# A fused attention and mixture-of-experts kernel: VectorE and GpSimd put in program order in the dense layers, with a shorter leaky step

## Chip, core and metric

The kernel runs on one core of a Trainium2 chip. The metric is the device time of one execution in microseconds (us); lower is better. TensorE multiplies, VectorE (DVE in the profile), ScalarE (ACT) and GpSimd (POOL) work element by element, and SyncE (SP) issues the transfers from memory.

## What is computed

Three stages follow each other on 2176 tokens of width 512.

```python
# 1 attention between 512 tokens and 32 state rows, 4 batches x 8 heads
xread = softmax(x @ state.T / 8) @ state;  sread = softmax(state @ x.T / 8) @ x
x = concat([xread, sread])                 # 4 * (512 + 32) = 2176 tokens, 512 wide
# 2 a dense two-layer net, 2048 hidden units, a leaky step with one slope a unit
h = x @ w_in
g = max(h, 0) + alpha * min(h, 0)
x = g @ w_out
# 3 eight experts of 1024 hidden units, weighted by P from 8 rounds of row and column scaling
out = sum(P[:, e:e+1] * (max(x @ w1[e], 0) @ w2[e]) for e in range(8))
```

Everything is float32. The kernel keeps the precision with two halves of each number: `hi` is a rounded copy that TensorE takes, `lo` is the rest, and each product is three matmuls (`hi` by `lo`, `hi` by `hi`, `lo` by `hi`). So every operand of TensorE costs one copy (ScalarE) and one subtraction (VectorE or GpSimd).

## The kernel before

The dense net, stage 2, is cut along its hidden units into 8 units `u` of 256 (two halves `f` of 128), and along the tokens into 5 chunks `c`: four of 512 tokens and a last one (c = 4, `CS`) of 128 state tokens. `program` (lines 805 to 813) lists the work as pairs: `layer1` of one chunk, then `layer2_first` of the chunk before it. A full chunk has two groups of six matmuls in `layer1` (one for each `f`) and four groups of six in `layer2_first` (one for each quarter `d` of the output). After each such group `run` calls `slot()`, which advances each of the side tasks ("lanes") by one step; a generator that yields n sleeps n slots. So a chunk is six slots, and a round of one `u` is 30.

What a chunk needs besides TensorE: `layer1` leaves a PSUM bank `ps` (three banks of the pool `ps_h`). ScalarE makes `r` = relu(h) and `v` = relu(-h) from it (lines 517, 518), VectorE makes `r` = r - alpha*v (line 519, the leaky step), and the closure `halves` makes `gh` on ScalarE (line 524) and `gl` on GpSimd (line 525). `halves` waits in the list `later` and is emitted one group of matmuls on. `layer2_first` leaves its sum in a bank of `ps_o` (three banks); VectorE adds it to `acc` (line 555; for u = 0 ScalarE copies, line 553). This is called the eviction of `d`. A bank can be filled again only after its eviction.

Two side tasks run under it. The lane "w" turns the weights of the next unit, which arrive as 64-bit numbers, into float32 and splits them: four pieces a round, each with `to_f32` (VectorE line 106, ScalarE 109 and 110, VectorE 112 and 115, GpSimd 118, VectorE 120) and `split_w` (ScalarE 135, GpSimd 136), and `load_next` issues the next transfer on SP. The lane "v" (`make_v`) multiplies the first layer's weights of the next unit by the attention's state, so that `layer1` can take the softmax weights as its input; it fills a bank of `ps_a` (two banks) and puts out two halves with `put_x` (ScalarE line 227, VectorE line 228).

Order: up to the entry (1, 2, 0) of `program` a planner orders all engines by a cost model of its own. From there on TensorE and ScalarE run in the order in which the code emits their instructions (`manual_schedule`, line 1038), while the planner still chooses the order of VectorE and GpSimd. Only in stage 3 (`experts`, line 1048) is VectorE in emitted order as well. Whatever chose the order, it is fixed before the run, and an engine takes its instructions one after the other.

Of the kernel before, what the change touches and what calls it, by code (L numbers as in the profile page):

```python
# [8 lines left out]
F32 = mybir.dt.float32  # L9
# [10 lines left out]
P = 128  # L20
# [24 lines left out]
def body(ctx: ExitStack, tc: tile.TileContext, xt_in, xn_in, stb, stk, wd, ws, alpha, wgate, out):  # L45
# [22 lines left out]
    ones = const.tile([P, P], F32, name="ones")  # L68
    rebias = const.tile([P, 1], F32, name="rebias")
    alpha_sb = const.tile([P, F1 // P], F32, name="alpha_sb")  # L70
    nalpha = const.tile([P, F1 // P], F32, name="nalpha")
    wg_raw = const.tile([P, KD, E], F32, name="wg_raw")
# [24 lines left out]
    def to_f32(u, j):  # L97
# [16 lines left out]
        )  # L114
        nc.vector.tensor_scalar(  # L115
            out=y.bitcast(I32), in0=y, scalar1=4095.0, scalar2=float(1 << 19), op0=ALU.min, op1=ALU.mult
        )
        nc.gpsimd.tensor_tensor(out=lo_w, in0=y.bitcast(I32), in1=lo_w, op=ALU.add)  # L118
# [184 lines left out]
    def read_state(b):  # L303
# [3 lines left out]
        for g in range(2):  # L307
            r2 = r2s[g]
            nc.vector.tensor_scalar(out=r2, in0=r2, scalar1=EPS, scalar2=None, op0=ALU.add)
            nc.vector.reciprocal(out=r2, in_=r2)  # L310
            nc.vector.tensor_scalar(out=a2[g], in0=a2[g], scalar1=r2, scalar2=None, op0=ALU.mult)
        yield 1
# [152 lines left out]
    def make_v(u):  # L465
# [4 lines left out]
        for bp in range(2):  # L470
# [3 lines left out]
            for j in range(2):  # L474
                ps = ps_a.tile([P, 2, NF, P], F32, tag="a", name=f"pv{u}_{bp}_{j}")
                for g in range(2):
                    k = 2 * g + j
                    for i, (s, w) in enumerate(((0, wl_t), (0, wh_t), (1, wh_t))):
                        nc.tensor.matmul(
                            ps[:, g], lhsT=st2[s][:, bp, g, j].rearrange("p h c -> p (h c)"),  # L480
                            rhs=w[u][:, :, k * P:(k + 1) * P], start=(i == 0), stop=(i == 2),
                        )
                for half in range(2):
                    h = slice(half * 64, half * 64 + 64)
                    v = v_of(u, 2 * bp + (half ^ j))
                    src = ps[h].rearrange("p g f c -> p g (f c)")
                    put_x(v[0][h], v[1][h], src)
                if j == 1:
                    v_done.add((u, bp))
                yield 2  # L490

    v_done = set()

    def layer1(u, c, f):
# [16 lines left out]
        for i, (w, x) in enumerate(terms):  # L511
            nc.tensor.matmul(ps, lhsT=w, rhs=x, start=(i == 0), stop=(i == len(terms) - 1))  # L512
        hi, lo = gh[:, f, :n], gl[:, f, :n]
        fa = u * NF + f
        r = tp.tile([P, S], F32, tag="r", name=f"r{u}_{c}_{f}", bufs=2)[:, :n]
        v = tp.tile([P, S], F32, tag="v", name=f"v{u}_{c}_{f}", bufs=1)[:, :n]
        nc.scalar.activation(out=r, in_=ps, func=AF.Relu)  # L517
        nc.scalar.activation(out=v, in_=ps, func=AF.Relu, scale=-1.0)  # L518
        nc.vector.scalar_tensor_tensor(  # L519
            out=r, in0=v, scalar=nalpha[:, fa:fa + 1], in1=r, op0=ALU.mult, op1=ALU.add  # L520
        )

# [3 lines left out]

        later.append(halves)

    def layer2_first(u, c, d):
# [7 lines left out]
        for f in range(NF):  # L537
            for wt, g in ((wh_t, gl), (wh_t, gh), (wl_t, gh)):
# [3 lines left out]
                i += 1  # L542
        for g, there, here in places(c):
            if g not in acc:
                new_acc(g)
            if c < CS:
                a, src = acc[g][:, d, there], ps[:, here]
            elif d == KD - 1:
                a, src = acc[g][:, :, there], po_t[False].rearrange("p (d n) -> p d n", d=KD)
            else:  # L550
                continue
            if u == 0:
                nc.scalar.activation(out=a, in_=src, func=AF.Copy)
            else:
                nc.vector.tensor_tensor(out=a, in0=src, in1=a, op=ALU.add)  # L555

# [258 lines left out]
    made = {}  # L815
    later, lanes = [], {"x": [], "state": [], "gate": [], "early": [], "sums": [], "blocks": [], "v": [], "w": []}
    wait = dict.fromkeys(lanes, 0)

    def advance(lane):
# [8 lines left out]
        return False  # L828

    def slot():  # L830
        for lane in lanes:
            if wait[lane] > 0:
# [33 lines left out]
    def weights(u, converted=0, first=5):  # L866

        yield first
        for j in range(NPIECE):
            if j >= converted:  # L870
                for _ in to_f32(u, j):
                    yield 1
                yield 2
            split_w(u, j)
            load_next(u, j)
            yield 2

# [15 lines left out]
    def start():  # L893
# [4 lines left out]
        nc.vector.memset(ones, 1.0)  # L898
        nc.vector.memset(rebias, -14336.0)
        warm(10)  # L900
        load_b(1)
# [16 lines left out]
        warm(30)  # L918
        nc.vector.tensor_scalar(out=nalpha, in0=alpha_sb, scalar1=-1.0, scalar2=None, op0=ALU.mult)
        lanes["x"] += [x0, x1, read_x(2), read_x(3)]  # L920
# [10 lines left out]
    def run(program):  # L931
        for kind, u, c in program:
            if kind == 1:
# [24 lines left out]
                for f in range(NF):  # L958
                    layer1(u, c, f)
                    while len(later) > 1:  # L960
                        later.pop(0)()
                    slot()
# [4 lines left out]
            else:  # L967
                while later and c == 0 and u == 0:
                    later.pop(0)()
                while (u, NPIECE - 1) not in split:  # L970
# [6 lines left out]
                for i in range(KD):  # L977
                    layer2_first(u, c, i)
                    if i == 1 and later:
                        later.pop(0)()  # L980
                    slot()
                while later:
                    later.pop(0)()
                if u == U1 - 1:
# [53 lines left out]
    with tc.manual_schedule(engines={mybir.EngineType.PE, mybir.EngineType.Activation}):  # L1038
        run(program[i:])
        flush("w")  # L1040
# [60 lines left out]
```

## Time and profile before

| | us |
|---|---|
| median of 3 runs | 1923.8 |
| lowest and highest of them | 1923.53, 1924.28 |
| the profiled execution, its own time | 1931.88 |
| span of that execution, first to last instruction | 1930.0 |
| stage 2 from `layer1` of u = 2 to the first matmul of stage 3 (177.3 to 477.5 of the span) | 300.2 |
| TensorE's matmuls over the span | 1852.3 busy, 96% |
| VectorE, ScalarE, GpSimd over the span | 64%, 39%, 64% busy |

The profiled execution took 8 us more than the median of the runs. Times inside it are counted from the span's start. Matmuls overlap each other, so a matmul's duration (0.39 us) is longer than the distance to the next one's start, and a busy TensorE is not yet one at its peak: what it needs is read from the distance between starts.

### The profile page before, as it was taken

Reading aid. Unit: us, or ns where it says so; the run is one execution under the profiler, and the core shown is the slowest. Engines: PE = TensorE matmul, PEld = TensorE weight load, DVE = VectorE, ACT = ScalarE, POOL = GpSimd, SP = SyncE. Lnnn points to the kernel's source line nnn. Section 1 sums busy time; section 2 is a strip of 40 time slices with the busy share of each in tenths; the row PEclk is TensorE's granted clock in tenths of the full one; section 3 lists DMA queues with packets and bytes.
Section 4 is the critical chain, followed back from the end, with each engine's and each line's share of the span. In section 5 each row is a group of like instructions: output and inputs, shape, how many; then the busy total and the mean of one; then the engine's idle time right before and its main releaser. Section 6 shows DMA issues by size and latency. Waiting matters only on the chain.

```text
span 1930.0 us, 26030 instructions
## 1 busy us (share of the span) xinstructions
PE 1852.3 (96%) x9544; PEld 1629.8 (84%) x9544; DVE 1229.7 (64%) x2048; ACT 756.3 (39%) x1389; POOL 1232.1 (64%) x1429
## 2 busy tenths in 40 slices
PE   7799898889989999999999999999999999999998
PEld 6687777767778989888889898888888898998997
DVE  6845777766586555556675555555566766666665
ACT  5656545554323333333343333333333333333332
POOL 4524444464756666666676666666666788888883
PEclk8799999999999999999999999999999999999999
DMA  5111111101112111221222222112221322222221
GB/s 213 44 50 55 43 36 43 44 22 33 61 50 66 66 66 67 72 70 66 70 80 92 66 66 66 66 66 67 75 67 55 121 78 80 84 87 78 77 88 50
DMA packets 66848, 132.53 MB, mean 69 GB/s; under 512 B 7712, under 2 KB 32800, under 8 KB 66720
## 3 DMA queue, kind: packets, MB, share of 16 engines
q1 hardware_dynamic: 66720, 130.86, 20.6%
q8 instruction: 75, 1.23, 0.3%
q14 instruction: 53, 0.43, 0.1%
HBM read 126.38 MB, written 4.46 MB: 68 GB/s over the span
## 4 chain that ended last, share of the span: by engine, by line
PE 80%; DVE 8%; ACT 3%; issue 3%; POOL 2%; DMA 0%; ACTq 0%; POOLq 0%; DVEq 0%
PE po L770 38%; PE py L711 14%; PE px L711 10%; PE pz L711 10%; PE po L539 3%; PE ph L512 3%; DVE r L519 2%; POOL raw L118 1%; ACT v L518 1%; DVE acc L555 1%; DVE raw L112 1%; PE psr L326 1%; DVE raw L120 1%; ACT r L517 1%; DVE y L115 1%
## 5 line engine op out<-in xcount | busy, mean ns | idle before, releaser
L792 DVE SCALAR_TENSOR_TENSOR oa<-po,pr,oa 128x512 f32<-128x512 f32 x509 | 382.0, 751 | 402.4 <-PE po L770 401.6
L648 POOL TENSOR_TENSOR wsl<-sum,wsh 128x256 fp32r<-128x256 f32 x384 | 282.9, 767 | 385.8 <-ACT wsh L646 362.1
L722 ACT ACTIVATE g2h<-c 128x384 fp32r<-128x384 f32 (+1 forms) x288 | 146.2, 508 | 849.1 <-DVE c L718 849.1
L770 PE MATMUL po<-w2h,g2h 128*128 128x512 f32 x1088 | 430.1, 395 | 0.0
L770 PE MATMUL po<-w2l,g2h 128*128 128x512 f32 x1088 | 429.6, 395 | 0.0
L770 PE MATMUL po<-w2h,g2l 128*128 128x512 f32 x1088 | 425.6, 391 | 1.2 <-DVE g2l L723 1.2
L648 POOL TENSOR_TENSOR w2l<-rw,w2h 128x512 fp32r<-128x512 f32 x192 | 247.8, 1310 | 10.4 <-ACT w2h L646 10.4
L770 PEld LDWEIGHTS po<-w2l,g2h 128*128 128x128 f32 x1088 | 204.3, 188 | 44.6
L770 PEld LDWEIGHTS po<-w2h,g2l 128*128 128x128 f32 x1088 | 204.6, 188 | 27.8 <-DVE g2l L723 1.7
L770 PEld LDWEIGHTS po<-w2h,g2h 128*128 128x128 f32 x1088 | 204.3, 188 | 24.7
L648 POOL TENSOR_TENSOR wal<-rw,wah 128x256 fp32r<-128x256 f32 x288 | 210.9, 759 | 0.0
L711 PE MATMUL px<-rB,wah 128*128 128x384 f32 (+1 forms) x768 | 189.0, 328 | 0.0
L711 PE MATMUL py<-rT,wsh 128*128 128x384 f32 (+1 forms) x768 | 188.8, 328 | 0.0
L525 POOL TENSOR_TENSOR gl<-r,gh 128x512 fp32r<-128x512 f32 (+1 forms) x80 | 92.2, 1155 | 150.0 <-ACT gh L524 142.6
L723 DVE SCALAR_TENSOR_TENSOR g2l<-c,g2h 128x384 fp32r<-128x384 f32 (+1 forms) x288 | 183.4, 637 | 0.1
L718 DVE TENSOR_TENSOR u<-py,p 128x384 f32<-128x384 f32 (+1 forms) x192 | 102.8, 535 | 118.0 <-PE py L711 52.7
L539 PE MATMUL po<-gl,wh 128*128 128x512 f32 (+1 forms) x320 | 124.1, 388 | 42.7 <-DVE acc L555 24.3
L711 PEld LDWEIGHTS px<-rB,wah 128*128 128x128 f32 x768 | 138.9, 189 | 14.0
L711 PEld LDWEIGHTS py<-rT,wsh 128*128 128x128 f32 x768 | 138.5, 189 | 8.5 <-DVE u L718 0.2
L658 POOL TENSOR_TENSOR sum<-rw 128x256 f32<-128x256 f32 x192 | 139.9, 748 | 6.2 <-DMA rw<-in_ws_dram 5.5
L711 PE MATMUL px<-rB,wal 128*128 128x384 f32 (+1 forms) x384 | 125.8, 328 | 2.8 <-POOL wal L648 2.8
L711 PE MATMUL py<-rT,wsl 128*128 128x384 f32 (+1 forms) x384 | 125.9, 328 | 0.0
(188 smaller groups left out, 3506.0 us busy)
## 6 DMA issues: line engine op xcount, KB each, us to landing
rw<-in_ws_dram SPq DMA_DIRECT2D x96, 512.0 KB, 3.5
rw<-in_ws_dram SPq DMA_DIRECT2D x96, 256.0 KB, 2.8
rw<-in_ws_dram SPq DMA_DIRECT2D x192, 128.0 KB, 2.7
raw<-in_wd_dram SPq DMA_DIRECT2D x29, 512.0 KB, 3.5
xt<-in_xt_dram SPq DMA_DIRECT2D x8, 512.0 KB, 8.1
xn<-in_xn_dram SPq DMA_DIRECT2D x16, 256.0 KB, 2.9
out_dram<-oa SPq DMA_DIRECT2D x16, 256.0 KB, 3.4
early_a<-in_wd_dram SPq DMA_DIRECT2D x2, 512.0 KB, 9.9
```

The lines of the kernel that those rows point to most:

```text
L512: nc.tensor.matmul(ps, lhsT=w, rhs=x, start=(i == 0), stop=(i == len(terms) - 1))
L519: nc.vector.scalar_tensor_tensor(out=r, in0=v, scalar=nalpha[:, fa:fa + 1], in1=r, op0=ALU.mult, op1=ALU.add)
L525: nc.gpsimd.tensor_tensor(out=lo, in0=r, in1=f32(hi), op=ALU.subtract)
L539: nc.tensor.matmul(ps, lhsT=w2(wt, u, f, d * P, P), rhs=g[:, f, :n], start=(i == 0), stop=(i == 3 * NF - 1))
L648: nc.gpsimd.tensor_tensor(out=lo[:, i], in0=src[:, i], in1=f32(hi[:, i]), op=ALU.subtract)
L658: nc.gpsimd.tensor_tensor(out=out, in0=x, in1=y, op=op)
L711: nc.tensor.matmul(bank[b], lhsT=w[:, k * P:(k + 1) * P], rhs=xf[:, j, k, :], start=(first and i == 0), stop=(i == 5), skip_group_check=True,)
L718: nc.vector.tensor_tensor(out=temp(name, tag, bufs), in0=bank[b], in1=t[x], op=ALU.add)
L722: nc.scalar.activation(out=hi, in_=src, func=AF.Relu)
L723: later.append(lambda: nc.vector.scalar_tensor_tensor(out=lo, in0=src, scalar=0.0, in1=f32(hi), op0=ALU.max, op1=ALU.subtract))
L770: nc.tensor.matmul(ps, lhsT=x[:, f, t * P:(t + 1) * P], rhs=w[:, f, :], start=(i == 0), stop=(i == 3 * NF - 1))
L792: nc.vector.scalar_tensor_tensor(out=a, in0=ps, scalar=p, in1=a, op0=ALU.mult, op1=ALU.add)
```

## The change

The change has six parts. (1) In the dense layers from entry (1, 2, 0) on, VectorE and GpSimd run in the order in which the code emits them. (2) A list `soon` with a counter, served by `tick()` at the start of each `slot()`, takes the place of `later` in the dense layers: the leaky step is emitted one slot after its matmuls, `halves` two slots after, an eviction one slot after. (3) The leaky step reads the PSUM bank itself: ScalarE makes r = relu(-h), VectorE makes h + (1 - alpha) * r; the second ScalarE pass and the tile `v` go, and `r` has three buffers. (4) In the weights' conversion the clamp and scaling on VectorE (line 115) become two ScalarE passes. (5) Conversion steps are two slots apart, with the rests after them shortened so that a piece still takes six slots; in `make_v` both copies are emitted first and both subtractions a slot later. (6) In the attention, the scaling of `a2` (line 311) goes from VectorE to ScalarE.

```diff
-        nc.vector.tensor_scalar(
-            out=y.bitcast(I32), in0=y, scalar1=4095.0, scalar2=float(1 << 19), op0=ALU.min, op1=ALU.mult
-        )
+        nc.scalar.activation(out=y, in_=y, func=AF.Relu, scale=-1.0, bias=full)
+        nc.scalar.activation(out=y.bitcast(I32), in_=y, func=AF.Copy, scale=-float(1 << 19), bias=4095.0 * (1 << 19))
...
-            nc.vector.tensor_scalar(out=a2[g], in0=a2[g], scalar1=r2, scalar2=None, op0=ALU.mult)
+            nc.scalar.activation(out=a2[g], in_=a2[g], func=AF.Copy, scale=r2)
...
+                parts = []
                 for half in range(2):
                     h = slice(half * 64, half * 64 + 64)
                     v = v_of(u, 2 * bp + (half ^ j))
-                    src = ps[h].rearrange("p g f c -> p g (f c)")
-                    put_x(v[0][h], v[1][h], src)
+                    parts.append((v[0][h], v[1][h], ps[h].rearrange("p g f c -> p g (f c)")))
+                for hi, lo, src in parts:
+                    nc.scalar.activation(out=hi, in_=src, func=AF.Copy)
+                yield 1
+                for hi, lo, src in parts:
+                    nc.vector.tensor_tensor(out=lo, in0=src, in1=f32(hi), op=ALU.subtract)
                 if j == 1:
                     v_done.add((u, bp))
-                yield 2
+                yield 1
...
-        nc.scalar.activation(out=r, in_=ps, func=AF.Relu)
-        nc.scalar.activation(out=v, in_=ps, func=AF.Relu, scale=-1.0)
-        nc.vector.scalar_tensor_tensor(
-            out=r, in0=v, scalar=nalpha[:, fa:fa + 1], in1=r, op0=ALU.mult, op1=ALU.add
-        )
+        nc.scalar.activation(out=r, in_=ps, func=AF.Relu, scale=-1.0)
+
+        def leak():
+            nc.vector.scalar_tensor_tensor(
+                out=r, in0=r, scalar=beta[:, fa:fa + 1], in1=ps, op0=ALU.mult, op1=ALU.add
+            )
...
-        later.append(halves)
+        soon.append([1, leak])
+        soon.append([2, halves])
...
+        if c < CS or d == KD - 1:
+            soon.append([1, evict])
...
+    def tick():
+
+        for entry in list(soon):
+            entry[0] -= 1
+            if entry[0] < 0:
+                soon.remove(entry)
+                entry[1]()
+
     def slot():
+        tick()
...
                 for _ in to_f32(u, j):
-                    yield 1
-                yield 2
+                    yield 2
+                yield 1
             split_w(u, j)
             load_next(u, j)
-            yield 2
+            yield 1
...
     with tc.manual_schedule(engines={mybir.EngineType.PE, mybir.EngineType.Activation}):
-        run(program[i:])
+        with tc.manual_schedule(engines={mybir.EngineType.DVE, mybir.EngineType.Pool}):
+            run(program[i:])
+            while soon:
+                tick()
```

## Rows read from the trace of the kernel before

**Rows 1.** Stretches: from:to, length, busy (instructions) of PE, PEld, DVE, ACT, POOL, clock, DMA, GB/s
```profile
25.00:82.80 57.80, 36.51 (x146) 28.89 (x147) 48.71 (x85) 36.31 (x67) 29.51 (x24) 0.68 0.15 50
...
292.40:341.10 48.70, 43.19 (x217) 34.64 (x217) 36.80 (x56) 26.11 (x50) 21.96 (x19) 1.00 0.14 44
...
391.50:477.50 86.00, 76.21 (x369) 61.89 (x368) 57.07 (x84) 41.64 (x80) 46.73 (x46) 0.94 0.08 25
477.50:1930.00 1452.50, 1437.35 (x7377) 1287.02 (x7376) 901.73 (x1526) 496.73 (x885) 1021.01 (x1242) 1.00 0.22 72
```

**Rows 2.** TensorE's timeline: start, duration (us), line, tiles, form; idle before, releaser
```profile
308.68 0.39 PE L539 MATMUL po<-gh,wl 128*128 128x512 f32 x1
...
309.59 0.28 PE L479 MATMUL pv<-wl,sth 128*128 128x256 f32 x1
...
310.30 0.40 PE L539 MATMUL po<-gl,wh 128*128 128x512 f32 x1
...
313.20 0.28 PE L512 MATMUL ph<-xsh,wh 128*128 128x128 f32 x1
313.31 0.27 PE L512 MATMUL ph<-xsh,wl 128*128 128x128 f32 x1
```

**Rows 3.** Waits in 177.3 to 477.5: who waited for whom, total us, times, longest
```profile
ACT wh L135 <- DVE raw L120: 40.4, 15, 3.9
...
PE po L539 <- DVE acc L555: 23.2, 20, 3.0
ACT v L227 <- DVE v L228: 19.6, 12, 4.0
...
PE po L539 <- POOL gl L525: 9.3, 11, 2.2
```

**Rows 4.** The timeline of four engines before one wait of TensorE
```profile
330.41 0.62 ACT L524 ACTIVATE gh<-r 128x512 fp32r<-128x512 f32 x1
...
331.79 1.30 POOL L118 TENSOR_TENSOR raw<-y,raw 128x512 int32<-128x512 int32 x1 [0.97 <-DVE y L115]
333.05 1.27 POOL L525 TENSOR_TENSOR gl<-r,gh 128x512 fp32r<-128x512 f32 x1
333.12 1.74 DVE L120 SCALAR_TENSOR_TENSOR raw<-raw 128x512 int32<-128x512 int32 x1 [1.42 <-POOL raw L118]
...
334.90 0.68 ACT L135 ACTIVATE wh<-raw 128x512 fp32r<-128x512 f32 x1 [3.87 <-DVE raw L120]
...
335.48 0.58 ACT L517 ACTIVATE r<-ph 128x512 f32<-128x512 f32 x1
...
338.92 0.68 DVE L555 TENSOR_TENSOR acc<-po,acc 128x512 f32<-128x512 f32 x1
...
339.66 0.50 PE L539 MATMUL po<-gl,wh 128*128 128x512 f32 x1 [1.59 <-DVE acc L555]
```

**Rows 5.** Groups by line and form, 177.3 to 477.5: count, busy us, mean ns, idle before
```profile
L519 DVE SCALAR_TENSOR_TENSOR r<-v,nalpha,r 128x512 f32<-128x512 f32 x48 | 41.7, 869 | 40.0 <-ACT v L518 40.0
L112 DVE SCALAR_TENSOR_TENSOR raw<-raw 128x512 int32<-128x512 uint16 x20 | 21.7, 1087 | 1.9 <-ACT raw L109 1.7
...
L115 DVE TENSOR_SCALAR y<-y 128x512 int32<-128x512 f32 x20 | 17.0, 848 | 0.0
...
L110 ACT ACTIVATE y<-y,rebias 128x512 f32<-128x512 int32 x20 | 14.2, 711 | 0.0
```

**Rows 6.** Two lines, each 177.3 to 477.5: durations min/median/max in ns, first and last start
```profile
L115 DVE TENSOR_SCALAR y<-y x20: 415/422/1517, 184.0 to 412.7; 128x512 int32<-128x512 f32 x20
...
L120 DVE SCALAR_TENSOR_TENSOR raw<-raw x20: 692/693/1745, 185.8 to 415.8; 128x512 int32<-128x512 int32 x20
```

**Rows 7.** The page: a group (busy us, mean ns, idle), a transfer (us to landing)
```profile
L792 DVE SCALAR_TENSOR_TENSOR oa<-po,pr,oa 128x512 f32<-128x512 f32 x509 | 382.0, 751 | 402.4 <-PE po L770 401.6
...
raw<-in_wd_dram SPq DMA_DIRECT2D x29, 512.0 KB, 3.5
```

**Rows 8.** TensorE's timeline in the first microseconds
```profile
56.41 0.80 PE L539 MATMUL po<-gl,wh 128*128 128x512 f32 x1 [7.75 <-POOL gl L525]
```

More of the change, by code (lines that the diff above doesn't have):

```diff
@@ L69, in body @@
     rebias = const.tile([P, 1], F32, name="rebias")
+    full = const.tile([P, 1], F32, name="full")
     alpha_sb = const.tile([P, F1 // P], F32, name="alpha_sb")
-    nalpha = const.tile([P, F1 // P], F32, name="nalpha")
+    beta = const.tile([P, F1 // P], F32, name="beta")
     wg_raw = const.tile([P, KD, E], F32, name="wg_raw")
@@ L514, in layer1 @@
         fa = u * NF + f
-        r = tp.tile([P, S], F32, tag="r", name=f"r{u}_{c}_{f}", bufs=2)[:, :n]
-        v = tp.tile([P, S], F32, tag="v", name=f"v{u}_{c}_{f}", bufs=1)[:, :n]
-        nc.scalar.activation(out=r, in_=ps, func=AF.Relu)
-        nc.scalar.activation(out=v, in_=ps, func=AF.Relu, scale=-1.0)
-        nc.vector.scalar_tensor_tensor(
-            out=r, in0=v, scalar=nalpha[:, fa:fa + 1], in1=r, op0=ALU.mult, op1=ALU.add
-        )
+        r = tp.tile([P, S], F32, tag="r", name=f"r{u}_{c}_{f}", bufs=3)[:, :n]
+        nc.scalar.activation(out=r, in_=ps, func=AF.Relu, scale=-1.0)
[3 more added lines that the diff above has]
+            )
         def halves():
@@ L542, in layer2_first, with evict @@
                 i += 1
[L543 to L555, printed above, removed]
+        bank = po_t[c < CS]
+        def evict():
+            for g, there, here in places(c):
+                if g not in acc:
+                    new_acc(g)
+                if c < CS:
+                    a, src = acc[g][:, d, there], bank[:, here]
+                else:
+                    a, src = acc[g][:, :, there], bank.rearrange("p (d n) -> p d n", d=KD)
+                if u == 0:
+                    nc.scalar.activation(out=a, in_=src, func=AF.Copy)
+                else:
+                    nc.vector.tensor_tensor(out=a, in0=src, in1=a, op=ALU.add)
+        if c < CS or d == KD - 1:
+            soon.append([1, evict])
     po_t = {}
@@ L815, in body @@
     made = {}
-    later, lanes = [], {"x": [], "state": [], "gate": [], "early": [], "sums": [], "blocks": [], "v": [], "w": []}
+    later, soon, lanes = [], [], {"x": [], "state": [], "gate": [], "early": [], "sums": [], "blocks": [], "v": [], "w": []}
     wait = dict.fromkeys(lanes, 0)
@@ L899, in start @@
         nc.vector.memset(rebias, -14336.0)
+        nc.vector.memset(full, 4095.0)
         warm(10)
@@ L918, in start @@
         warm(30)
-        nc.vector.tensor_scalar(out=nalpha, in0=alpha_sb, scalar1=-1.0, scalar2=None, op0=ALU.mult)
+        nc.vector.tensor_scalar(out=beta, in0=alpha_sb, scalar1=-1.0, scalar2=1.0, op0=ALU.mult, op1=ALU.add)
         lanes["x"] += [x0, x1, read_x(2), read_x(3)]
@@ L959, in run @@
                     layer1(u, c, f)
-                    while len(later) > 1:
-                        later.pop(0)()
                     slot()
@@ L967, in run @@
             else:
-                while later and c == 0 and u == 0:
-                    later.pop(0)()
                 while (u, NPIECE - 1) not in split:
@@ L978, in run @@
                     layer2_first(u, c, i)
-                    if i == 1 and later:
-                        later.pop(0)()
                     slot()
-                while later:
-                    later.pop(0)()
                 if u == U1 - 1:
```

## The prediction

> **What bounds the kernel now.** Read the stretches first [rows 1]. Stage 3 keeps TensorE busy for 1437 of 1452 us; the change doesn't touch it, and it is taken as it is. The dense stage from u = 2 on (177.3 to 477.5, 300.2 us) is another matter: in one round (292.4 to 341.1) TensorE is busy for 43.2 of 48.7 us, VectorE for 36.8, ScalarE for 26.1 and GpSimd for 22.0. No engine is full; engines wait for each other.
>
> How much is lost is read from the distances between matmul starts [rows 2]. Four matmuls of 512 columns take 309.59 - 308.68 = 0.91 us, so 0.228 each and 1.37 for a slot of six; those of 128 columns start 0.11 apart; six of `make_v` take 310.30 - 309.59 = 0.71. By the loops the stage holds 864 of the first kind, 312 of the second, 20 groups of the third and 1.4 us of gate logits: 197.0 + 34.5 + 14.2 + 1.4 = 247.1 us. So 300.2 - 247.1 = **53 us are lost**, 8.8 in each of six rounds. (For one round: 96 + 48 of the first kind, 48 of the second, four groups: 41.0 us of 48.7.)
>
> The waits tell where [rows 3]: TensorE waits 23.2 us for evictions and 9.3 for `gl`; the rest is refilling after each wait, and the clock, whose mean is 0.94 between its levels of 1.2 and 2.4 GHz from 391.5 on [rows 1]. Behind the evictions stands a chain [rows 4]: GpSimd's line 118 ends at 333.09; VectorE's line 120 takes 1.74 us, since GpSimd starts `gl` beside it; ScalarE, in program order, sat idle for 3.87 us until line 120 let it do `wh`; only then come the relus; and an eviction starts at 338.92, for which TensorE waits until 339.66. Such waits for line 120 cost ScalarE 40.4 us in 15 cases, and its second copy in `make_v` waits 19.6 us for VectorE's first subtraction [rows 3].
>
> **The change, part by part.** *Work per engine.* VectorE loses line 115 (four a round at 0.848 us [rows 5]) and the leaky step, at 0.869 now, is taken at 0.751, a step of the same kind with one PSUM operand [rows 7]: 36.8 - 3.4 - 0.9 = 32.5 us of a 41.0 us round. ScalarE loses a pass (0.58 [rows 4]) for each half chunk and gains two for each piece, bounded by 0.58 and 0.711 [rows 4, 5]; the latter is taken, being the pass on the same tile: 26.1 - 8 x 0.58 - 0.6 + 8 x 0.711 = 26.6. GpSimd stays at 22.0. All three fit under 41.0, so nothing but order can hold TensorE up.
>
> The Trainium skill (Perfetto Trace Analysis, Optimizing Scalar/DVE Operations) speaks against both moves: it gives VectorE a fixed cost some 65 ns higher from PSUM than from SBUF, and says that an operation with a VectorE performance mode is faster there. By it the 48 leaky steps would cost about 3 us more, an estimate, and line 115 should stay. The rows disagree on the first (0.751 against 0.869) and on the second only partly: undisturbed, line 115 takes 0.415, but its longest took 1.517 [rows 6].
>
> *Order, steady chunk.* Leaky step, conversion and eviction now come a slot after what feeds them. Count from the end of the second half's matmuls, with their 0.17 us of pipeline: relu done at 0.8, leaky step at 1.5, `gh` (0.62) at 2.2, two conversion passes at 3.6, `gl` (1.3) at 3.5, line 118 at 4.9, line 120 (0.693 undisturbed [rows 6]) at 5.6. VectorE puts the evictions of d = 0 and 1 in between, and its next use of line 120 is ScalarE's `wh` in the next chunk, at 6.9 or later: no wait. `gl` is needed at 8.2. The 40.4 us of waiting on ScalarE go, and so does the 19.6 in `make_v`, where both copies precede both subtractions.
>
> *Order, short chunk.* After the first chunk of a round, TensorE has only 24 short matmuls (2.7 us) before the next `layer1` (2.7). ScalarE has lines 109 and 110 ahead of `gh`: `gh` of both halves at 2.8 and 3.4, the new passes at 4.8; GpSimd `gl` at 4.1 and 5.4, line 118 at 6.7; line 120 at 7.4. `gl` is just in time (needed at 5.4 and 6.1). Queued behind line 120 on VectorE are the short chunk's eviction (8.1), two leaky steps with line 106 between them (taken at 0.42 as line 115, a step of its kind: 10.0), and the eviction of d = 0 (10.7). TensorE needs that bank at 5.4 + 3 x 1.37 = 9.5: a wait of 1.2, with refilling 1.5 us.
>
> *Slots with `make_v`.* For eight slots a round, VectorE has in every two slots two subtractions, a conversion step and two evictions or leaky steps, 4 x 0.68 + 0.7 to 1.09 [rows 4, 5] = 3.4 to 3.8, against 2 x 1.37 + 0.71 = 3.44 of TensorE. Up to 0.4 too much four times; an eviction may be late by two slots less its own 0.68 and the pipeline, 1.9. Bounds 0 and 1.6 us; I take 1.0.
>
> *Sum of the stage.* A steady round keeps 1.5 + 1.0 = 2.5 of 8.8 us; four of them 10. In the last two rounds the planner's VectorE also has the block differences for stage 3, which are not moved; I leave 11 of 17.6. So 21 of 53 stay: **32 us gained** (bounds: 53, and 20 if each steady round keeps twice as much and the last two 13).
>
> *Free of cost.* The transfers that `load_next` puts on SP go out a slot (1.4 us) later; they land in 3.5 us [rows 7] and are used 13 slots on. If they had to be waited for, it would be 1.4 us a piece. The leaky step holds its PSUM bank for a slot more; the third bank covers that.
>
> *First 177 us.* Here the planner still orders everything, and no row shows its choice. Best: the longest wait goes, -7.75 [rows 8]. Worst: the eight pieces of the first two units each add 2 x 0.711 - 0.422 = 1.0 us to the path, and eight scalings of `a2` 0.62 each: +13. I take 0: from 25 to 82.8 VectorE is the fuller engine (48.7 against 36.3 [rows 1]) and is the one relieved.
>
> Against the profiled execution: 1931.9 - 32 = 1899.9 us. It stands 8 us over the median; the parts that change are the same in both, so 1923.8 - 32 = **1892 us**.
>
> **The rivals.** *A held queue on VectorE (slower).* Line 120 sits in emitted order ahead of leaky steps and evictions, and its input now hangs on two more ScalarE passes. What such a place costs an engine in fixed order is seen on ScalarE today: up to 3.9 us, 2.7 in the mean [rows 3]. If VectorE waits W at each of 20 pieces, an eviction behind it is late by W + 0.69 - 1.9. With 11 us elsewhere the stage loses more than now once 20 x (W - 1.21) + 11 > 53, so from W = 3.3 on; at 3.9 it is 65, time **1936**. For it: the short chunk comes to a wait of that kind. Against: pieces are two slots a step now, and the steady chunk shows none. The Trainium skill says of these engines that their queues are strictly first in, first out (PSUM — Partial Sum Buffer, Engine vs sequencer instructions); by that rule this rival lives.
>
> *Twice the waits.* VectorE's spare 8.5 us a round is eaten, since GpSimd's steps lengthen lines 106, 112 and 120 (line 112 takes 1.087 in the mean [rows 5]) in the full slots. Rounds keep 5 and the last two 14: 34 of 53, **1905**.
>
> *All waits go.* The short chunk is eased because ScalarE's passes take 0.58, and the last rounds gain as the others: 6 of 53 stay, **1877**.
>
> *It does not do what it says.* The planner's order was near the emitted one, and what counted was the chain's length: one pass (0.58) less for `gl`, but 1.42 - 0.85 more for line 118. These cancel: **1923**.
>
> **How the numbers follow.** Forecast 0.50, all waits go 0.17, twice the waits 0.16, no effect 0.06, held queue 0.11. Faster by over 0.2% (about what a measurement of this kernel can tell from no change): 0.83; within: 0.06; slower: 0.11. The range leaves out the held queue and the far ends: low 1923.8 - 53 = 1871, high 1923.8 - 20 + 13 = 1917.
>
> **What the profile would show.** Right: rounds of some 43.5 us where they were 48.7; ScalarE's wait for line 120 below 15 us; no leaky step over 0.8 us; one wait for an eviction of about 1.2 us left a round, in the chunk after the short one; stage 3 as long as before. Wrong: VectorE idle before line 120 for over 3 us a piece, with evictions behind it; or a start that lasts past 183 us to `layer1` of u = 2.

## The result, and the profile after

The changed kernel takes 1893.8 us (median of 4 runs, 1891.8 to 1898.4) against 1924.0 us: a ratio of 0.984, 95% interval 0.982 to 0.987. The forecast was 1892 us with a range of 1871 to 1917. The profiled execution is the slowest of the four, 1898.44 us, with a span of 1896.7. The profiled execution of the kernel before is 8 us above its median too, so the two spans differ by 33.3 us and the medians by 30.2.

The stretches of the changed kernel, in the columns of [rows 1]. Stage 2 from `layer1` of u = 2 now runs from 180.9 to 447.3.

```profile
25.00:82.80 57.80, 34.27 (x148) 28.68 (x149) 39.01 (x65) 41.32 (x77) 24.48 (x20) 0.66 0.15 50
...
238.60:281.20 42.60, 41.37 (x217) 35.17 (x216) 31.03 (x52) 27.11 (x49) 22.18 (x19) 1.00 0.15 50
...
366.40:447.30 80.90, 74.55 (x369) 60.90 (x368) 52.95 (x81) 37.96 (x69) 48.75 (x47) 0.96 0.09 27
447.30:1896.70 1449.40, 1434.44 (x7377) 1284.33 (x7375) 900.92 (x1526) 496.89 (x885) 1023.48 (x1242) 1.00 0.22 72
```

A round went from 48.7 us (the one in [rows 1]; they vary from 48.3 to 50.0) to 42.6, the stretch that ends stage 2 from 86.0 to 80.9, and stage 3 from 1452.5 to 1449.4 [rows 1]. Over the span: the start is 3.6 us longer (180.9 against 177.3), stage 2 is 33.8 us shorter (266.4 against 300.2), stage 3 is 3.1 us shorter; together 33.3, the difference of the spans.

Two lines give all of stage 2, before and after:

```profile
177.30:477.50 300.20, 266.00 (x1305) 214.59 (x1304) 217.26 (x319) 156.22 (x298) 141.99 (x123) 0.97 0.12 37
```

```profile
180.90:447.30 266.40, 254.01 (x1305) 213.19 (x1305) 186.11 (x298) 156.03 (x277) 143.94 (x123) 0.99 0.13 42
```

TensorE's idle time fell by 21.8 us (34.2 to 12.4), and the same matmuls were busy for 12.0 us less. Part of that is the clock: it stood at 1.2 GHz for 17.1 us of stage 2 before and for 6.8 us after. Matmuls of 512 columns then start 0.43 us apart (428.48 and 428.90 in the changed kernel) in place of 0.228, so about half of such a stretch is lost: an estimate of 5 of the 33.8 us.

The waits of the changed kernel in stage 2 (who waited for whom, total us, times, longest), to be laid beside [rows 3]:

```profile
DVE raw L121 <- POOL raw L119: 33.9, 10, 4.3
ACT wh L136 <- DVE raw L121: 30.4, 15, 2.5
...
PE po L547 <- DVE acc L564: 10.8, 8, 2.7
...
PE po L547 <- POOL gl L532: 1.6, 3, 0.7
```

TensorE's waits fell from 23.2 + 9.3 to 10.8 + 1.6 us. But ScalarE still waits 30.4 us for line 120 (121 in the new file), where it waited 40.4. So that wait, with which the prediction's reading of the chain began, is mostly still there, and TensorE's waits fell all the same.

One wait of TensorE is left in each round. Here are TensorE's and VectorE's timelines before it (start, duration, line, tiles, idle before):

```profile
271.30 0.28 PE L547 MATMUL po<-gh,wl 128*128 128x128 f32 x1
...
279.71 0.50 PE L547 MATMUL po<-gl,wh 128*128 128x512 f32 x1 [1.23 <-DVE acc L564]
```

```profile
275.32 0.69 DVE L121 SCALAR_TENSOR_TENSOR raw<-raw 128x512 int32<-128x512 int32 x1 [4.29 <-POOL raw L119]
275.93 0.68 DVE L564 TENSOR_TENSOR acc<-po,acc 128x512 f32<-128x512 f32 x1
276.53 0.74 DVE L526 SCALAR_TENSOR_TENSOR r<-r,beta,ph 128x512 f32<-128x512 f32 x1
277.19 1.21 DVE L107 TENSOR_SCALAR y<-raw 128x512 int32<-128x512 int32 x1
278.32 0.73 DVE L526 SCALAR_TENSOR_TENSOR r<-r,beta,ph 128x512 f32<-128x512 f32 x1
278.98 0.68 DVE L564 TENSOR_TENSOR acc<-po,acc 128x512 f32<-128x512 f32 x1
```

It is the queue that the prediction wrote out for the short chunk: the conversion step held for GpSimd, then the short chunk's eviction, two leaky steps with a conversion step between them, and the eviction for which TensorE stands still for 1.23 us. VectorE keeps its order: the short chunk's last matmul started at 271.30 and took 0.28 us, but its eviction stood behind line 121 and ran at 275.93.

The leaky step, one line of each kernel, durations min/median/max in ns (the first fence is the kernel before, the second the changed one):

```profile
L519 DVE SCALAR_TENSOR_TENSOR r<-v,nalpha,r x60: 339/752/1799, 180.1 to 465.2; 128x512 f32<-128x512 f32 x48, 128x128 f32<-128x128 f32 x12
```

```profile
L526 DVE SCALAR_TENSOR_TENSOR r<-r,beta,ph x60: 336/737/750, 183.2 to 435.0; 128x512 f32<-128x512 f32 x48, 128x128 f32<-128x128 f32 x12
```

None of the 60 is over 0.750 us, though GpSimd worked beside 32 of them for more than 0.1 us; before, the longest took 1.799, and all 15 steps over 0.8 us had GpSimd at work beside them. The Trainium skill (SBUF — State Buffer, Who interferes with whom) says that a VectorE instruction with at most one input in SBUF, outside the two-port modes, does not contend with GpSimd, and that one with two inputs there contends with a GpSimd instruction that reads SBUF. The trace agrees.

### The profile page after: what moved, and what is told of

It reads as the page before. It is cut to its first block, busy times and chain, and to the rows that moved or that the text cites. A ratio compares the mean times of both kernels' runs of the same rounds, so it can differ in the third digit from the quotient of the medians.

```text
span 1896.7 us, 25997 instructions
## 1 busy us (share of the span) xinstructions
PE 1838.0 (97%) x9544; PEld 1628.7 (86%) x9544; DVE 1192.9 (63%) x2009; ACT 765.1 (40%) x1381; POOL 1235.6 (65%) x1429
## 3 DMA queue, kind: packets, MB, share of 16 engines
q8 instruction: 75, 1.23, 0.3%
## 4 chain that ended last, share of the span: by engine, by line
PE 87%; DVE 5%; POOL 2%; ACT 2%; issue 2%; DMA 1%; SPq 0%; POOLq 0%; ACTq 0%; DVEq 0%
PE po L782 39%; PE py L723 15%; PE px L723 10%; PE pz L723 10%; PE po L547 7%; PE ph L518 4%; PE pv L480 1%; PE psr L327 1%; POOL gl L532 1%; POOL raw L119 1%; DVE r L526 1%; PE psc L248 1%; DMA raw<-in_wd_dram 1%; DVE acc L564 0%; DVE y L107 0%
## 5 line engine op out<-in xcount | busy, mean ns | idle before, releaser
L547 PE MATMUL po<-gl,wh 128*128 128x512 f32 (+1 forms) x320 | 121.1, 379 | 12.4 <-DVE acc L564 10.8
```

The costliest lines, as they stand in the source:

```text
L547: nc.tensor.matmul(ps, lhsT=w2(wt, u, f, d * P, P), rhs=g[:, f, :n], start=(i == 0), stop=(i == 3 * NF - 1))
```

## The experiments

The theory of the prediction was "order": no engine is full, so the gain is that VectorE and GpSimd run in emitted order, with each step a slot behind. The first rival was "work": the cheaper steps carry it. Each kernel below was timed against the kernel before in runs on the same chip, where that took 1925.7 to 1926.4 us, and the ratios refer to those runs; "stage 2" is the stretch from `layer1` of u = 2 to stage 3 in its profiled execution, "round" the distance between `layer1` of u = 4 and of u = 5 (chunk 0). Rounds differ within a kernel before (48.3 to 50.0), in e2 (47.3 to 56.3) and in e6 (42.4 to 50.7).

| kernel | us | ratio to before, 95% interval | start of u = 2 | stage 2 | round |
|---|---|---|---|---|---|
| before | 1924.0 | 1 | 177.3 | 300.2 | 50.0 |
| changed | 1893.8 | 0.984 (0.982 to 0.987) | 180.9 | 266.4 | 42.6 |
| e1 changed, planner's order | 1892.0 | 0.982 (0.981 to 0.983) | 176.2 | 261.8 | 42.4 |
| e2 before, emitted order | 1948.0 | 1.011 (1.009 to 1.012) | 175.4 | 318.5 | 52.8 |
| e3 changed, clamp on VectorE | 1896.3 | 0.984 (0.983 to 0.986) | 174.7 | 269.3 | 43.3 |
| e4 changed, old leaky step | 1908.6 | 0.990 (0.988 to 0.992) | 181.1 | 277.0 | 44.5 |
| e5 before, new leaky step alone | 1903.7 | 0.989 (0.987 to 0.990) | 179.0 | 272.3 | 45.4 |
| e6 changed, conversion a slot apart | 1907.2 | 0.990 (0.989 to 0.992) | 172.8 | 278.1 | 50.7 |
| e7 changed, `make_v` paired | 1943.5 | 1.009 (1.007 to 1.011) | 188.6 | 303.3 | 51.3 |
| e8 changed, no lag, planner's order | 1888.0 | 0.980 (0.979 to 0.982) | 179.7 | 252.5 | 41.1 |
| e9 before, three cheaper steps | 1910.3 | 0.992 (0.990 to 0.993) | 182.2 | 275.3 | 46.2 |
| e10 as e5, an idle ScalarE pass | 1910.6 | 0.992 (0.990 to 0.993) | 175.9 | 284.5 | 47.3 |
| e11 as e8, clamp on VectorE | 1887.6 | 0.980 (0.978 to 0.982) | 177.6 | 259.0 | 42.0 |
| e12 changed, no lag, emitted order | 1901.0 | 0.987 (0.985 to 0.989) | 183.2 | 266.1 | 42.5 |

### Is it the order?

e1, the changed kernel with the planner's order back:

```diff
-        with tc.manual_schedule(engines={mybir.EngineType.DVE, mybir.EngineType.Pool}):
-            run(program[i:])
-            while soon:
-                tick()
+        run(program[i:])
+        while soon:
+            tick()
```

> The changed kernel, but the planner again orders VectorE and GpSimd in the dense layers; the cheaper steps and the lag of a slot in the code stay. Theory 'order': the gain sits in the order, so the stage from layer1 of u = 2 to stage 3 (266.4 us in the changed kernel, 300.2 before) goes back to 288 or more, time 1912 or more, rounds of 47 us and up. Rival 'work': what counted is the shorter work on VectorE and the shorter chains; the stage stays under 277, time 1893 to 1904.

Measured 1892.0 us, stage 2 261.8, rounds 42.4. The theory "order" falls for its first half, the emitted order: nothing is lost, and stage 2 is even 4.6 us shorter. The lag is still in this kernel; e8 takes it out.

e2, the kernel before with emitted order and nothing else:

```diff
-        run(program[i:])
+        with tc.manual_schedule(engines={mybir.EngineType.DVE, mybir.EngineType.Pool}):
+            run(program[i:])
```

> The kernel before with nothing changed but the order: VectorE and GpSimd in emitted order in the dense layers, each step emitted where it was, not a slot behind. Theory 'order, with the lag': an eviction now stands ahead of work that is ready, and line 120 one slot behind line 118, so VectorE waits in its queue; the stage keeps most of its waits or gets more, 290 to 315 us, time 1912 to 1938. If emitted order alone were enough, the stage is under 280 and the time under 1905. Rival 'work': no step is cheaper, so nothing changes, 1920 to 1928.

Measured 1948.0 us, slower than before by 1.1%, stage 2 318.5. Time and stage lie beyond the worse end that was written down. Emitted order alone puts each eviction and each conversion step ahead of work that is ready; three of its waits in stage 2:

```profile
PE po L539 <- DVE acc L555: 35.4, 16, 4.7
POOL raw L118 <- DVE y L115: 34.4, 16, 3.3
...
DVE raw L120 <- POOL raw L118: 13.5, 10, 2.7
```

TensorE waited 23.2 us for evictions before [rows 3], and GpSimd 8.6 us for line 115. So emitted order makes VectorE late in the old places of the code. But it is not the slower rival of the prediction, a VectorE held at line 120: there it waits 13.5 us, less than the 17.4 of the kernel before. What VectorE waits longer for is TensorE at evictions (20.7 us against 10.9) and ScalarE at the leaky step (49.5 against 43.0).

### Is it the cheaper steps?

e3 puts the clamp back on VectorE in the changed kernel.

```diff
-        nc.scalar.activation(out=y, in_=y, func=AF.Relu, scale=-1.0, bias=full)
-        nc.scalar.activation(out=y.bitcast(I32), in_=y, func=AF.Copy, scale=-float(1 << 19), bias=4095.0 * (1 << 19))
+        nc.vector.tensor_scalar(
+            out=y.bitcast(I32), in0=y, scalar1=4095.0, scalar2=float(1 << 19), op0=ALU.min, op1=ALU.mult
+        )
```

> The changed kernel with the clamp and scaling of the conversion back on VectorE, one step in place of two ScalarE passes. Theory 'order': VectorE has 31.0 us of work in a round of 42.6 and takes 4 x 0.42 to 0.85 more without harm, and line 118 starts 1.0 us earlier, so the one wait of 1.2 us a round shrinks: 1885 to 1895. Rival 'work': taking it off VectorE carried part of the gain, 1900 or more.

Measured 1896.3 us: between the two expectations. Stage 2 is 2.9 us longer than in the changed kernel, the start 6.2 us shorter in the profiled executions, the median 2.4 us longer with ranges that overlap. The clamp is not what carries the gain.

e4 puts the old leaky step back in the changed kernel, with its tile `v` and two buffers of `r`.

```diff
-        nc.scalar.activation(out=r, in_=ps, func=AF.Relu, scale=-1.0)
+        nc.scalar.activation(out=r, in_=ps, func=AF.Relu)
+        nc.scalar.activation(out=v, in_=ps, func=AF.Relu, scale=-1.0)
...
-                out=r, in0=r, scalar=beta[:, fa:fa + 1], in1=ps, op0=ALU.mult, op1=ALU.add
+                out=r, in0=v, scalar=beta[:, fa:fa + 1], in1=r, op0=ALU.mult, op1=ALU.add
```

> The changed kernel with the old leaky step: two ScalarE passes, then VectorE on two tiles in SBUF. Theory 'order': ScalarE has 27.1 us in a round of 42.6 and VectorE 31.0; 4.6 to 5.2 us more on ScalarE and steps of up to 1.8 us on VectorE when GpSimd runs beside it make the wait after the short chunk longer, by up to 1.2 us a round: 1893 to 1902. Rival 'work': the shorter step carried the gain, 1908 or more.

Measured 1908.6 us, half of the gain gone, stage 2 10.6 us longer. That speaks for "work", and for one step of it.

e5 does the reverse: the new leaky step alone in the kernel before, emitted where it was.

```diff
-        nc.scalar.activation(out=r, in_=ps, func=AF.Relu)
-        nc.scalar.activation(out=v, in_=ps, func=AF.Relu, scale=-1.0)
+        nc.scalar.activation(out=r, in_=ps, func=AF.Relu, scale=-1.0)
...
-            out=r, in0=v, scalar=nalpha[:, fa:fa + 1], in1=r, op0=ALU.mult, op1=ALU.add
+            out=r, in0=r, scalar=nalpha[:, fa:fa + 1], in1=ps, op0=ALU.mult, op1=ALU.add
```

(`nalpha` holds 1 - alpha here, and `r` has three buffers.)

> The kernel before with the new leaky step alone (one ScalarE pass, VectorE reads the PSUM bank, three buffers of r); all else, also where it is emitted, as before. Undoing the step in the changed kernel cost 10.6 us of stage 2. Theory 'additive work': it gives the same here, 1910 to 1918. Rival 'place': the waits of the kernel before (ScalarE for line 120, evictions behind others) hide most of it, 1918 to 1927.

Measured 1903.7 us: a larger gain than either expected. Stage 2 is 27.9 us shorter than before in the profiled executions, with everything else, the planner too, as it was; the medians differ by less, 20.4 us (22.1 in runs on the same chip). Four of its waits in stage 2:

```profile
ACT wh L135 <- DVE raw L120: 40.7, 15, 3.9
...
DVE r L517 <- ACT r L516: 17.2, 23, 1.4
...
PE po L537 <- DVE acc L553: 9.7, 9, 2.0
...
PE po L537 <- POOL gl L523: 1.9, 2, 1.2
```

ScalarE waits for line 120 for 40.7 us, just as before (40.4 [rows 3]), while TensorE's waits for evictions and `gl` fell from 23.2 and 9.3 us to 9.7 and 1.9. So that wait was not what TensorE paid these 28 us for; whether it has a part in the 25 that are still lost (272.3 - 247.1) is not shown.

e10 asks what it is in the leaky step. It is e5 with the second ScalarE pass kept, its result overwritten.

```diff
+        nc.scalar.activation(out=r, in_=ps, func=AF.Relu)
         nc.scalar.activation(out=r, in_=ps, func=AF.Relu, scale=-1.0)
```

> The kernel before with the new leaky step alone, and ahead of its ScalarE pass a second one whose result is overwritten (r = relu(h), then r = relu(-h)), so ScalarE and the chain have the two passes of the kernel before, while VectorE reads the PSUM bank and no tile v with a single buffer is waited for. Without that pass it took 1903.7. Theory 'pass': the gain of 22 us is the pass that left the chain: 1915 or more. Rival 'buffer and port': it is ScalarE's wait for the single buffer of v (16.5 us in 21 cases before) and VectorE's slower step beside GpSimd (0.869 against 0.737): 1908 or less.

Measured 1910.6 us, between the two; the medians of e10 and e5 differ by 6.9 us. In stage 2 the pass takes back 12.2 of the 27.9 us (284.5 against 272.3). Its waits, to be laid beside those of e5, show the way from ScalarE to TensorE:

```profile
DVE r L518 <- ACT r L517: 36.1, 39, 2.3
...
PE po L538 <- DVE acc L554: 15.0, 14, 2.4
...
PE po L538 <- POOL gl L524: 8.2, 11, 1.9
```

VectorE waits longer for ScalarE's pass, and TensorE for `gl` nearly as long as before (8.2 against 9.3). The pass also adds to ScalarE's load; a pass off the chain was not tried. The other 15.7 us stay gained. They belong to what the extra pass does not touch: VectorE's step with one operand in PSUM, never held up by GpSimd, the single buffer of `v`, for which ScalarE waited 16.5 us before, and the third buffer of `r`. These were not told apart.

e9 is the kernel before with all three cheaper steps and nothing else: e5 with the clamp's two ScalarE passes (the removed lines of e3's diff put in) and the `a2` scaling on ScalarE.

```diff
-            nc.vector.tensor_scalar(out=a2[g], in0=a2[g], scalar1=r2, scalar2=None, op0=ALU.mult)
+            nc.scalar.activation(out=a2[g], in_=a2[g], func=AF.Copy, scale=r2)
```

> The kernel before with the three cheaper steps (leaky step, clamp on ScalarE, a2 on ScalarE), and no other part: the planner orders VectorE and GpSimd, nothing is emitted later, conversion and make_v as before. The leaky step alone gave 1903.7; all but lag and emitted order gave 1888.0. Theory 'spacing': the other 16 us are due to the wider conversion and the unpaired make_v, which keep ScalarE, itself in emitted order, from waiting (40.7 us for line 120, 36.7 in make_v with the leaky step alone): 1899 or more. Rival 'clamp': they are due to the clamp that left VectorE: 1885 to 1893.

Measured 1910.3 us, 6.7 us more than the leaky step alone, as "spacing" had it. About half of that is in stage 2 (3.0 us) and half in the start (3.2), where all of the `a2` scalings lie. So with the conversion a slot apart and `make_v` paired, moving the clamp to ScalarE gains nothing in stage 2. GpSimd now waits for the second pass (8.6 us for line 115 before):

```profile
POOL raw L118 <- ACT y L117: 28.5, 16, 3.3
```

So "work" alone isn't the answer either: the spacing has its own part.

### Is it the places in the code?

e6 sets the conversion's steps one slot apart again, in the changed kernel.

```diff
                 for _ in to_f32(u, j):
-                    yield 2
-                yield 1
+                    yield 1
+                yield 2
             split_w(u, j)
             load_next(u, j)
-            yield 1
+            yield 2
```

> The changed kernel with the conversion's steps one slot apart again (rests 1, 1, then 2 and 2). Theory 'place': line 120 is emitted one slot after the add on GpSimd that feeds it, which takes until two slots on, so VectorE waits in every piece with evictions behind it: stage 2 from 266.4 to 275 or more, 1900 to 1915. Rival 'additive work': no work is added, 1890 to 1897.

Measured 1907.2 us, stage 2 278.1, as expected of "place"; TensorE waits 15.2 us for evictions in place of 10.8. VectorE's wait for GpSimd's add is now in all 20 pieces:

```profile
DVE raw L121 <- POOL raw L119: 40.4, 20, 3.4
```

e7 pairs copy and subtraction in `make_v` again.

```diff
-                for hi, lo, src in parts:
-                    nc.scalar.activation(out=hi, in_=src, func=AF.Copy)
-                yield 1
-                for hi, lo, src in parts:
-                    nc.vector.tensor_tensor(out=lo, in0=src, in1=f32(hi), op=ALU.subtract)
+                for hi, lo, src in parts:
+                    put_x(hi, lo, src)
                 if j == 1:
                     v_done.add((u, bp))
-                yield 1
+                yield 2
```

> The changed kernel with copy and subtraction in make_v paired and emitted together, as before. ScalarE's second copy then waits for VectorE's first subtraction (34 us of such waits before, 19.6 and 14.3). Theory 'place': that holds ScalarE and the relus behind it in eight slots of a round, 0.7 to 2 us a round, 1897 to 1906. Rival 'additive work': 1890 to 1897.

Measured 1943.5 us, slower than before, stage 2 303.3: far beyond what was written down. The two halves lie in one PSUM tile, and in the trace ScalarE and VectorE take turns on it, each waiting for the other. The timeline of both:

```profile
321.27 0.67 DVE L229 TENSOR_TENSOR v<-pv,v 64x512 fp32r<-64x512 f32 x1
321.98 0.59 ACT L228 ACTIVATE v<-pv 64x512 fp32r<-64x512 f32 x1 [2.30 <-DVE v L229]
...
322.60 0.69 DVE L229 TENSOR_TENSOR v<-pv,v 64x512 fp32r<-64x512 f32 x1 [0.66 <-ACT v L228]
...
329.53 0.50 PE L544 MATMUL po<-gl,wh 128*128 128x512 f32 x1 [3.61 <-DVE acc L561]
```

In emitted order everything behind it on VectorE waits too, and TensorE stands still for 3.61 us, once a round. The clock falls with it: around each of the four such waits it stands at 1.2 GHz for 10.3 to 13.7 us, the stretch of stage 2 has a mean of 0.92 (of 2.4 GHz), the changed kernel's rounds 1.00. Of the 36.9 us that stage 2 is longer, 20.7 are matmuls that were busy longer (274.7 against 254.0) and 16.2 are idle time.

```profile
188.60:491.90 303.30, 274.71 (x1305) 229.93 (x1304) 188.33 (x298) 155.36 (x277) 143.53 (x123) 0.92 0.11 37
```

The Trainium skill's rule that these queues are strictly first in, first out (PSUM — Partial Sum Buffer, Engine vs sequencer instructions) agrees with the eviction above that ran at 275.93, 4.3 us after its matmuls, behind line 121; e6 and e7 show what such a place costs.

### Is it the lag?

e8 takes the lag out of the changed kernel and lets the planner order VectorE and GpSimd (the diff of e1 and this one):

```diff
-        soon.append([1, leak])
-        soon.append([2, halves])
+        leak()
+        soon.append([1, halves])
...
-            soon.append([1, evict])
+            evict()
```

> The changed kernel, but leaky step, halves and eviction emitted a slot earlier (at once, one slot, at once) and VectorE and GpSimd ordered by the planner. With the lag and the planner it took 1892.0. Theory 'place': ScalarE, in emitted order, meets gh before the leaky step is done, and the planner puts evictions ahead of what is ready; rounds of 44 to 47 us in place of 42.4, 1900 to 1915. Rival 'additive work': the lag does nothing, 1889 to 1896.

Measured 1888.0 us, the best with e11. Rounds take 41.1 us, which is what the matmul distances ask for (41.0), and stage 2 252.5, its matmuls 248.8 busy:

```profile
179.70:432.20 252.50, 248.81 (x1306) 211.66 (x1305) 186.48 (x297) 156.05 (x277) 142.03 (x123) 1.00 0.14 45
```

TensorE's waits for evictions are down to 3.7 us, and none for `gl` is listed. With the planner the lag costs 9.3 us of stage 2 (e1, 261.8); the medians differ by 4.0. The expectation that ScalarE would meet `gh` too early was wrong.

e12 is e8's second diff alone: no lag, but emitted order.

> The changed kernel without the lag, with VectorE and GpSimd in emitted order: the fourth corner beside 1893.8 (lag, emitted), 1892.0 (lag, planner) and 1888.0 (no lag, planner). Theory: the lag pays only for the emitted order, since VectorE then stands at an eviction until TensorE has ended that group: rounds of 44 or more, 1902 or more. Rival: the lag costs as much in either order, 1886 to 1893.

Measured 1901.0 us (1895.7 to 1904.9), stage 2 266.1 against 266.4 with the lag. Neither expectation holds: in stage 2 the lag is worth nothing in emitted order, and rounds stay at 42.5. The medians differ by 7 us, but the ranges overlap; the profiled execution has a start that is 2.3 us longer. What the lag does to the total in that order is open.

e11 is e8 with the clamp back on VectorE (e3's diff).

> The changed kernel with no lag and the planner's order (1888.0), and the clamp back on VectorE. If the move of the clamp carries part of the gain: 1891 or more, rounds over 42. If VectorE has room for it, rounds stay at 41.1 and the first 177 us, where ScalarE was full, get 2 to 5 us shorter: 1883 to 1888.

Measured 1887.6 us, the same as e8. The rounds (42.0) speak for the first expectation, the time for the second. In the profiled executions stage 2 is 6.5 us longer (259.0) and the start 2.1 us shorter; that of e8 is its fastest run, 3.2 us below its median, so how the two add up to the same median is not shown.

### What the parts are worth

A path through the kernels gives each part its share of stage 2 (one profiled execution each) and of the median time:

| from, to | what is added | stage 2, us | median, us |
|---|---|---|---|
| before, e5 | leaky step | -27.9 | -20.4 |
| e5, e9 | clamp (and `a2`, in the start) on ScalarE | +3.0 | +6.7 |
| e9, e8 | conversion two slots apart, `make_v` unpaired, `halves` of the second half one group earlier | -22.8 | -22.3 |
| e8, e1 | lag of a slot | +9.3 | +4.0 |
| e1, changed | VectorE and GpSimd in emitted order | +4.6 | +1.8 |
| before, changed | all | -33.8 | -30.2 |

Two steps carry the gain, and the other three give a third of it back. The third row holds three changes at once (the kernel before emits the second `halves` of a chunk two groups on, not one). They were not told apart there; the first two were taken out singly in emitted order, in e6 and e7. The 1.8 us of emitted order in the median are within the spread of the runs. On another path the shares differ: taken out of the changed kernel, the leaky step is worth 10.6 and the clamp 2.9. What is shown is that emitted order and lag are not the source, and that without them the kernel is faster (1888.0 against 1893.8).

## Why the prediction was right, and where its reasons were wrong

*Right.* The loss: 53 us of waits were counted in stage 2 and 21 left; 266.4 - 247.1 = 19.3 stayed. The work per engine in a round came out at 31.0, 27.1 and 22.2 us where 32.5, 26.6 and 22.0 had been worked out. The short chunk: a wait of 1.2 us for the eviction of d = 0, one a round, was forecast and 1.23 was measured, behind the same queue (its terms offset each other: line 106 took 1.21 us beside GpSimd where 0.42 had been put down, and line 120 ended earlier than counted). The last two rounds' stretch gained 5.1 us (86.0 to 80.9); 6.6 had been put down. No leaky step took over 0.8 us. So the sum held because the waits that would be left were forecast well; it says nothing on which part removed the others. As far as the cause goes that was named for the gain, the agreement of the time is luck.

*Sizes.* The slots with `make_v` were given 1.0 us a round; of 42.6 - 41.0 = 1.6 us the short chunk's wait with its refilling takes about 1.4, so some 0.2 is left. Rounds were forecast at 43.5. The start was set at 0 and came out 3.6 us longer in the profiled execution, inside its bounds: from 25 to 82.8 ScalarE is now the fuller engine (41.3 us against 39.0), where VectorE had been (48.7 against 36.3 [rows 1]). The start lies between 172.8 and 188.6 us in the kernels of the table. It goes with TensorE's clock: over the start its mean is 0.91 in e2, e3 and e6 (172.8 to 175.4), 0.89 in the kernel before and 0.87 or less in the kernels from 180.9 us on. In the changed kernel one such stretch follows a wait of TensorE for `make_v`'s subtraction (the first line), which the kernel before does not have:

```profile
169.44 0.36 PE L480 MATMUL pv<-wl,sth 128*128 128x256 f32 x1 [2.33 <-DVE al L493]
```

```profile
170.40:177.30 6.90, 6.90 (x27) 6.14 (x27) 3.08 (x6) 3.31 (x10) 2.88 (x4) 0.51 0.48 154
```

In the three pairs that differ by the clamp (changed and e3, e8 and e11, e9 and e5, the last with `a2`) the start is 2.1 to 6.2 us longer with the clamp on ScalarE; which part brings the wait is not shown.

*Wrong: the cause.* The step that failed is the sentence that nothing but order can hold TensorE up, since all engines' work fits in a round. From it the leaky step was priced at 0.9 us of VectorE's work a round; its shorter path only entered the count of the new order, without a price of its own, and the whole gain was given to the new places and order. e1 shows that emitted order brought nothing (-4.6 us if taken away), e8 the same of the lag (-9.3 with the planner), e5 that the leaky step alone takes 27.9 us out of stage 2 and 20 out of the median. What is left of "order" is part (5), the new spacing of the conversion and of `make_v` (e9 to e8, -22.8 together with the earlier `halves`). Work that fits in the round can still lie on the path from `ph` to `gl` and to the evictions behind it; e10 shows it, where an idle pass on a ScalarE that is busy for little over half of the stretch costs 12.2 us:

```profile
175.90:460.40 284.50, 259.65 (x1306) 211.75 (x1305) 208.78 (x319) 160.48 (x298) 140.27 (x123) 0.99 0.12 40
```

*Wrong: the wait that was followed.* ScalarE's 40.4 us of waiting for line 120 were to go, with under 15 left. 30.4 are left in the changed kernel and 40.7 in e5, which is 20 us faster than before. It was a wait on an engine with time to spare. The count of the steady chunk gave line 120 no wait either; one of its three pieces a round waits 2.5 us. With the planner's order and the new spacing ScalarE's wait does fall under 15 (14.7 in e1, 13.0 in e8), so it goes with the spacing; what it costs TensorE by itself is open.

*The 19.6 us in `make_v`.* They went, as forecast, and e7 shows that in emitted order they had to: pairing costs 36.9 us of stage 2 there, more than the wait itself, because VectorE is then held as well and the clock falls.

*The Trainium skill against the change.* By the fixed costs that the prediction took from the Trainium skill (Perfetto Trace Analysis, Optimizing Scalar/DVE Operations) the leaky step would have become dearer; it takes 0.741 us in the mean where it took 0.869 [rows 5]. On its second point, that line 115 should stay on VectorE, the runs are divided: with the clamp back the time is 2.4 us longer (e3, ranges overlap) or the same (e11), while on the old spacing moving it costs 3.0 us of stage 2 (e9). The group of the changed kernel in stage 2:

```profile
L526 DVE SCALAR_TENSOR_TENSOR r<-r,beta,ph 128x512 f32<-128x512 f32 x48 | 35.4, 741 | 14.5 <-ACT r L523 14.4
```

*The rivals.* The held queue's deciding wait, 3.3 us a piece, is exceeded (4.2 to 4.3 us) in the short chunk's piece only, one a round; over all 20 pieces VectorE waits 33.9 us, 1.7 a piece. It decides in no kernel here: the mean is 0.7 a piece in e2, 2.0 in e6, and e7 has the changed kernel's wait at that line to the tenth:

```profile
DVE raw L121 <- POOL raw L119: 33.9, 10, 4.3
```

So the slow times of e2 and e7 have other causes, given above, and its 1936 was not put to the test. "All waits go" (6 of 53 left, 1877) is reached in stage 2 by e8: 252.5 - 247.1 = 5.4. The rival "it does not do what it says" came nearest to the cause: that emitted order changes little (e1) and the chain's length counts (e5, e10). It went wrong in taking the shorter and the longer chain to cancel.

## What to carry to other kernels

A change that bundles a cheaper step with a new order can land on the forecast time for the wrong reason: take the order away and leave the step, and the reverse, before crediting either. An engine that is half idle can still carry the path, so price a removed pass by the chain it leaves, not only by its engine's load, and check whether the wait that looks longest is felt by the engine that sets the time. Where the order of both engines is fixed, copies and subtractions of one PSUM tile are better emitted as two runs than in pairs (e7); for the planner's order that was measured only together with the wider conversion.

## What had not been expected of the hardware

The prediction took the new leaky step at 0.751 us, but not where its gain would come from. With nothing on GpSimd beside them, the old step (both operands in SBUF) took up to 0.755 us and the new one (one operand in PSUM) up to 0.750. Beside GpSimd the old one took up to 1.799 and the new one still no more than 0.750. So reading the PSUM bank a second time was no dearer than reading a copy in SBUF, and it kept its time.

Some waits of TensorE cost more than their length: after the one of 2.33 us in the start of the changed kernel the clock stood at 1.2 GHz for 6.9 us, and around those of 3.6 us in e7 for 10.3 us and more. Not every such wait did: after one of 2.82 us at 465.4 in the changed kernel it stayed at 2.4 GHz.
